# Wide products in the block passes of w1, a shared bank for two narrow ones, and weight sums made four steps at a time

## The chip, the cores and the metric

The kernel runs on one core of one Trainium2 chip. The time is device time in microseconds (us). Three runs of the kernel before took 515.21, 515.64 and 515.76 us; their median, 515.64 us, is the time before.

## The reference

The reference has two residual blocks over x (2048 tokens of 512 channels). The first is a linear attention with 32 heads; it is the same in both kernels. The second mixes tokens:

```
h  = x + attention(layernorm(x))
u  = gelu(w1^T · layernorm(h) + b1)       # w1: 2048 x 1792
h2 = h + (w2^T · u + b2)                  # w2: 1792 x 2048
```

All data are fp32. Every matmul operand is split into a high part (rounded to the type that TensorE takes, fp32r) and a low part (the rest), and a product is made of three: high with high, high with low, low with high.

## The kernel before

After the attention, the kernel walks through 96 numbered steps (`STEPS`). A step takes one tile of weights: 2 blocks of 128 rows by 256 columns. Steps 0 to 7 are pass 2 of w1, a plain one (kind "v"); steps 8 to 31 are passes 3, 4 and 5, the block passes (kind "u"), 8 steps each; steps 32 to 39 are pass 6, plain again; steps 40 to 95 are w2's (kind "y"). Passes 0 and 1 of w1 are filled in between the attention's work. This document is about steps 8 to 31.

In a block pass the 2x2 block product of a step is made of 7 products of 128x128 weights with 256 columns (a Winograd form of Strassen's scheme, P1 to P7) instead of 8. For that the weights need sums: of the 4 loaded blocks (slots 1 to 4 of `wraw`), VectorE makes slots 0, 5 and 6 and a new slot 1, four adds (`w_sums`, L801, L802, L803, L805), for two steps at a time. Then `w_parts` splits all 7 slots: ScalarE writes the high part (L66), VectorE subtracts it for the low part (L67), into one of three rotating tiles `wp` (`ws[n % 3]`). The activations have their sums too (`h_sums`, L738 and L739; `h_parts`, tiles `cb`), made for the last token tiles while the passes already run.

TensorE's work of a step is `products`: seven calls of `narrow`, each three matmuls of 256 columns (L989). They accumulate over the 8 steps of a pass into four PSUM banks a, b, c and d of 512 columns: P1 and P6 share a, P5 and P4 share b, P3 and P2 share c, P7 has the first half of d. Even and odd passes use different banks: an even pass takes the four of pool `ps_b`, an odd one two of `ps_f` and two of `ps_q`. At a pass's end `u_out` combines the banks: one copy on ScalarE (L1018) and five operations on VectorE (L1019 to L1028). Two steps later comes the gelu (L1033).

`wide`, which w2's steps use for four of their seven products, does the same product in two matmuls: the high weights with 512 columns (high and low activations side by side, L996), and the low weights with 256 (L998). It needs a whole bank for one product.

The order of everything is written by hand: all engines take their instructions in the order in which the program lists them. Step n runs `step(n)` (TensorE), then what is listed for n - 0.5, then `prepare(n + 2)`, which is `w_parts(n + 2)` and perhaps `w_sums`, then what is listed for n:

```python
for j, n in enumerate((0, 1, 2, 3, 5, 9, 12), 1):
    at(n - 1.5 if j > 3 else n - 0.5, h_sums, j)
    at(n, h_parts, j)
```

`U_ADDS` lists the steps at which the sums of a finished pass's u are made: two or three copies on ScalarE (L950), then a transfer that adds, issued by GpSimd (L951).

Of the kernel before, what the change touches and what calls it, by code (L numbers as in the profile page):

```python
# [9 lines left out]
F32 = mybir.dt.float32  # L10
F32R = mybir.dt.float32r
AF = mybir.ActivationFunctionType
ALU = mybir.AluOpType
# [4 lines left out]
P = 128  # L18
S, D, H, DH, F = 2048, 512, 32, 16, 1792
# [14 lines left out]
PLAIN = 2  # L34
KINDS = "vuuuv"
HD = D // 2
# [6 lines left out]
def block_kernel(ctx: ExitStack, tc: tile.TileContext, x, xT, wT, phic, wo, w1, b1, w2, b2,  # L43
                 kvmask, ident_in, out):
    nc = tc.nc
# [710 lines left out]
    Y0 = (NP - PLAIN) * (NT // 2)  # L756
# [36 lines left out]
    def w_sums(g):  # L793

        if 2 * g >= len(STEPS) or STEPS[2 * g][0] == "v":
            return
        plain = STEPS[2 * g][0] == "y"
        raw = BLOCK[g // 2 % 2] if plain else RAW[g]
        added = ADDED(2 * g)
        if not added:  # L800
            nc.vector.tensor_add(raw[:, :, 0], raw[:, :, 3], raw[:, :, 1])  # L801
        nc.vector.tensor_add(raw[:, :, 5], raw[:, :, 0], raw[:, :, 2])  # L802
        nc.vector.tensor_add(raw[:, :, 6], raw[:, :, 4], raw[:, :, 5])  # L803
        if not added:
            nc.vector.tensor_add(raw[:, :, 1], raw[:, :, 1], raw[:, :, 2])  # L805
# [10 lines left out]
        split(PARTS[n][0][:, k], PARTS[n][1][:, k], RAW[n // 2][:, n % 2, k], nc.vector)  # L816

    CB_FIRST = (0, 1, 2, 3)
    U_ADDS = {0: (5, 7, 9), 1: (6, 8, 10), 2: (11, 13, 15), 3: (19, 21, 23), 4: (28, 30, 32), 5: (34, 35.5, 37)}
    HELD = (44,)  # L820
    T_WORK = {5: 39.5}
    U_WORK = {0: 26, 1: 28, 2: 30, 3: 32, 4: 34, 5: 38, 6: 41}
# [162 lines left out]
    def narrow(o, n, m, x, opens, closes):  # L985

        wh_, wl_ = PARTS[n]
        for i, (w, y) in enumerate(((wh_, 0), (wh_, 1), (wl_, 0))):
            nc.tensor.matmul(o, w[:, m[0]], x[:, y], start=opens and i == 0, stop=closes and i == 2, skip_group_check=True)  # L989

    def wide(n, x, first, last, *products):


        wh_, wl_ = PARTS[n]
        for o, m in products:
            nc.tensor.matmul(o, wh_[:, m[0]], x(m[1]), start=first, stop=False, skip_group_check=True)  # L996
        for o, m in products:
            nc.tensor.matmul(o[:, 0], wl_[:, m[0]], x(m[1])[:, 0], start=False, stop=last, skip_group_check=True)  # L998
# [4 lines left out]
    def new_bank(pool):  # L1003
        return pool.tile([P, 2, HD], F32, name="py", tag="pu")

    def four_banks(i):
        return [new_bank(q) for q in ((ps_b,) * 4, (ps_f, ps_f, ps_q, ps_q))[i]]

    def products(n, banks, x, first, last):
        a, b, c, d = banks  # L1010
        for o, m, opens in ((a[:, 0], P1, True), (a[:, 1], P6, False), (d[:, 0], P7, True), (b[:, 0], P5, True),
                            (b[:, 1], P4, False), (c[:, 0], P3, True), (c[:, 1], P2, False)):
            narrow(o, n, m, x(m[1]), first and opens, last)

    def firsts(banks):
        a, b, c, d = banks
        tmp = wqp.tile([P, 4, HD], F32, name="tmp", tag="small")
        nc.scalar.activation(tmp[:, 1], a[:, 0], AF.Copy)  # L1018
        nc.vector.tensor_sub(tmp[:, 2], a[:, 1], tmp[:, 1])  # L1019
        nc.vector.tensor_sub(tmp[:, 3], tmp[:, 2], d[:, 0])  # L1020
        nc.vector.scalar_tensor_tensor(tmp[:, 0], b[:, 0], -1.0, tmp[:, 2], op0=ALU.mult, op1=ALU.subtract)
        return tmp[:, 0:2], tmp[:, 3].unsqueeze(1).to_broadcast([P, 2, HD])

    def u_out(p, banks):
        e, u3 = firsts(banks)
        U[p] = o = ur.tile([P, 4, HD], F32, name="u")
        nc.vector.tensor_add(o[:, 0:2], banks[1], u3)
        nc.vector.tensor_add(o[:, 2:4], banks[2], e)  # L1028

    def u_gelu(p):  # L1030
        for i in range(2):
# [9 lines left out]
    def wide_step(n, sp, p):  # L1041
        t = 2 * sp
        if p == 0:
            b3, b2 = [new_bank((ps_f, ps_q)[sp % 2]) for _ in range(2)]
            BK[:] = [new_bank(ps_b) for _ in range(4)] + [b3, b2]
        b16, b7, b5, b4, b3, b2 = BK
        first, end = p == 0, p == NP - 1

        def x(m):
            return UB[p, m]  # L1050

        def ws_(*products):
            wide(n, x, first, end, *products)

        w3, w2, w5, w4 = (b3, P3), (b2, P2), (b5, P5), (b4, P4)
        if first:
            ws_(w3, w2)
        elif not end:
            ws_(w3, w2, w5, w4)
        narrow(b16[:, 0], n, P1, x(1), first, end)  # L1060
        narrow(b16[:, 1], n, P6, x(5), False, end)
        narrow(b7[:, 0], n, P7, x(0), first, end)
        if first:
            ws_(w5, w4)
        if not end:
            return []
        ws_(w4, w5)
        ws_(w3, w2)
# [12 lines left out]
        nc.scalar.activation(lows[:, 3], b4[:, 1], AF.Copy)  # L1081
        tile_sum(0, 1, b4[:, 0], u3)
        add(l5, b5[:, 0], l5)
        add(e0, l5, u2)
        nc.scalar.activation(lows[:, 0], b3[:, 1], AF.Copy)  # L1085
        nc.scalar.activation(lows[:, 1], b2[:, 1], AF.Copy)
        tile_sum(0, 0, l5, u3)
        tile_sum(1, 0, b3[:, 0], e0, ALU.subtract)
        tile_sum(1, 1, b2[:, 0], e1)
        return [(t, 1, lows[:, 3:4]), (t, 0, ot[:, 0:2]), (t + 1, 0, ot[:, 2:4]), (t + 1, 0, lows[:, 0:2])]  # L1090

    def last_step(n, sp, p):
        t = 2 * sp
        if p == 0:
            b3, b2 = [new_bank((ps_f, ps_q)[sp % 2]) for _ in range(2)]
            BK[:] = [new_bank(ps_b) for _ in range(4)] + [b3, b2]
        b16, b7, b5, b4, b3, b2 = BK
        end = p == NP - 1
        if NP - 3 <= p < NP - 1:
            return []  # L1100
        places = [(b16[:, 0], P1, True), (b16[:, 1], P6, False), (b7[:, 0], P7, True), (b5[:, 0], P5, True),
                  (b4[:, 0], P4, True), (b3[:, 0], P3, True), (b2[:, 0], P2, True)]
        for o, m, opens in places if end else places[5:] + places[:5]:
            for k in range(2 if end else 0, -1, -1):
                narrow(o, n - k, m, UB[p - k, m[1]], opens and p == 0, end and k == 0)
        if end:
            last_sums(t, HB)
        return []
# [34 lines left out]
    def step(n):  # L1143

        kind, i, j = STEPS[n]
        if kind == "u":
            if j == 0:
                BANKS[0] = four_banks(i % 2)
            products(n, BANKS[0], lambda m: NB[j][m], j == 0, j == NT // 2 - 1)
            if j == NT // 2 - 1:  # L1150
                b = list(BANKS[0])
                later(0, lambda: u_out(i, b))
                later(2, lambda: u_gelu(i))
        elif kind == "v":
            if j == 0:
                PU[i] = [ps_b.tile([P, D], F32, name="pu", tag="pu") for _ in range(2)]
            wh_, wl_ = PARTS[n]
            for k in range(2):
                for c in range(2):
                    m, t = 1 + 2 * k + c, 2 * j + k  # L1160
                    mm3(PU[i][c], wh_[:, m], wl_[:, m], HN[t][:, 0], HN[t][:, 1], t == 0, t == NT - 1)
            if j == NT // 2 - 1:
                for c in range(2):
                    (later(0, lambda c=c: gelu(2 * i + c, PU[i][c])) if i < NP - 1 else gelu(2 * i + c, PU[i][c]))
        else:
            o = (last_step if i == NT // 2 - 1 else wide_step)(n, i, j)
            STORES.extend(o)
# [8 lines left out]
    def at(n, f, *args):  # L1176
        PENDING.setdefault(n, []).append(lambda: f(*args))

    for j, n in enumerate((0, 1, 2, 3, 5, 9, 12), 1):
        at(n - 1.5 if j > 3 else n - 0.5, h_sums, j)  # L1180
        at(n, h_parts, j)
    for p in range(PLAIN):
# [33 lines left out]
    def prepare(m):  # L1216

        if m >= len(STEPS):
            return
        w_parts(m)  # L1220
        made.add(m)
        if m >= Y0:
            if m % 4 == 2 and m > Y0 + 3:
                w_sums(m // 4 * 2 + 2)
        elif m % 2 == 0 and m + 2 < Y0:
            w_sums(m // 2 + 1)
        if m ^ 1 in made:
            load_raw(m // 2 + 4)
            add_raw(m // 2 + 3)
# [69 lines left out]
```

## Time and profile before

| | |
|---|---|
| time, median of three runs | 515.64 us |
| span of the profiled execution | 513.1 us |
| TensorE (PE) busy | 507.8 us, 99% |
| weight loads (PEld) busy | 441.7 us, 86% |
| VectorE (DVE) busy | 438.4 us, 85% |
| ScalarE (ACT) busy | 310.6 us, 61% |
| GpSimd (POOL) busy | 261.1 us, 51% |
| granted TensorE clock | 1.000 |

The span runs from the first to the last instruction of one profiled execution; the time of a run also holds what lies around the span. The profile has no time of its own for that execution beside its span; the median of the runs is 2.5 us above it. Busy time of PE counts matmuls that overlap, each for its whole length (0.28 us for one of 256 columns), so the distance between two starts, not the length, is what a matmul costs in a row of them.

### The profile page before, as it was taken

The page shows a single profiled execution, that of the slowest core. Times are in us where ns is not written, and L with a number is a line of the kernel's source. Part 1 is how long each engine was busy: PE and PEld are TensorE (multiplying, and loading weights), DVE is VectorE, ACT ScalarE, POOL GpSimd, SP SyncE. Part 2 cuts the span into 40 slices and gives each one's busy share as a digit, 9 for nine tenths or more (in the row PEclk, how much of TensorE's full clock was granted, in tenths as well). Part 3 has the DMA queues.
Part 4 walks back from the last instruction along what each step waited for, and adds up shares of the span by engine and source line. Part 5 has one row for each costly group of instructions (what it writes and reads, how often), then busy time and mean ns, then how long its engine had stood idle before and what let it go on. Part 6 is the DMA issues. An engine that isn't in the chain of part 4 may idle for free.

```text
span 513.1 us, 10496 instructions
## 1 busy us (share of the span) xinstructions
PE 507.8 (99%) x4024; PEld 441.7 (86%) x4024; DVE 438.4 (85%) x746; ACT 310.6 (61%) x557; POOL 261.1 (51%) x212
## 2 busy tenths in 40 slices
PE   8999999999999999999999999999999999999997
PEld 8888888888877777777788999998899999999997
DVE  6799889989887899699877898898799889868983
ACT  6999863525267878867676754577655444434530
POOL 3579997876999999985200421202323212211220
PEclk9999999999999999999999999999999999999999
DMA  8642301010123234354325775545677797668734
GB/s 308 217 144 84 103 22 42 1 65 21 42 64 103 67 100 145 127 169 132 95 69 185 150 159 125 133 115 151 173 164 147 181 199 167 122 153 190 169 51 85
DMA packets 53266, 63.35 MB, mean 123 GB/s; under 512 B 4832, under 2 KB 39904, under 8 KB 53216
## 3 DMA queue, kind: packets, MB, share of 16 engines
q1 hardware_dynamic: 44288, 51.90, 32.5%
q0 software_dynamic: 8640, 10.62, 14.9%
q8 instruction: 31, 0.51, 0.4%
q10 hardware_dynamic: 288, 0.17, 0.1%
q14 instruction: 19, 0.16, 0.1%
HBM read 48.39 MB, written 11.14 MB: 116 GB/s over the span
## 4 chain that ended last, share of the span: by engine, by line
PE 95%; DVE 2%; ACT 1%; DMA 1%; issue 0%; POOL 0%; DVEq 0%
PE py L989 25%; PE py L996 9%; PE pu L71 9%; PE pu L72 8%; PE pu L73 8%; PE py L998 4%; PE pk_ps L71 3%; PE pk_ps L72 3%; PE pk_ps L73 3%; PE pv L73 3%; PE pv L71 3%; PE pv L72 3%; PE po L71 3%; PE po L73 2%; PE po L72 2%; PE pn L616 2%
## 5 line engine op out<-in xcount | busy, mean ns | idle before, releaser
L66 ACT ACTIVATE wp<-wraw 128x896 fp32r<-128x896 f32 (+1 forms) x96 | 82.4, 895 | 68.3 <-DVE wraw L805 23.9
L67 DVE TENSOR_TENSOR wp<-wraw,wp 128x896 fp32r<-128x896 f32 (+1 forms) x96 | 95.5, 1019 | 14.9 <-ACT wp L66 14.6
L989 PE MATMUL py<-cb,wp 128*128 128x256 f32 x678 | 92.6, 283 | 0.0
L989 PEld LDWEIGHTS py<-cb,wp 128*128 128x128 f32 x678 | 86.1, 191 | 0.0
L1039 POOL DMA_DIRECT2D out<-u x28 | 24.8, 963 | 89.8 <-ACT u L1085 28.9
L951 POOL DMA_DIRECT2D tt<-u x14 | 13.4, 960 | 60.6 <-ACT tt L950 34.5
L490 POOL TENSOR_TENSOR ez<-eq,zB 128x1024 f32<-128x1024 f32 x16 | 38.4, 2406 | 3.8 <-ACT zB L550 3.8
L219 POOL TENSOR_TENSOR pk<-pk,sk 128x1024 f32<-128x1024 f32 x16 | 31.1, 1947 | 11.3 <-DVE sk L218 10.1
L996 PE MATMUL py<-cb,wp 128*128 128x512 f32 x126 | 36.1, 394 | 0.0
L514 POOL TENSOR_TENSOR eq<-eq,w 128x1024 f32<-128x1024 f32 x16 | 32.4, 2025 | 3.5 <-DVE w L511 3.5
L223 POOL TENSOR_TENSOR zacc<-zacc,pk 128x1024 f32<-128x1024 f32 x13 | 31.4, 2412 | 0.5
L989 PE MATMUL py<-hs,wp 128*128 128x256 f32 x216 | 30.0, 283 | 0.0
L989 PEld LDWEIGHTS py<-hs,wp 128*128 128x128 f32 x216 | 27.8, 192 | 0.1
L195 ACT ACTIVATE pk<-pk,r 128x1024 f32<-128x1024 f32 x16 | 18.4, 1149 | 15.0 <-DVE pk L173 14.4
L989 PE MATMUL py<-uf,wp 128*128 128x256 f32 x198 | 26.6, 283 | 0.0
L71 PE MATMUL pu<-wq,xs 128*128 128x512 f32 x64 | 26.1, 409 | 0.0
L71 PE MATMUL pu<-hs,whl 128*128 128x512 f32 x64 | 26.0, 406 | 0.0
L71 PE MATMUL po<-woh,oh 128*128 128x512 f32 x64 | 25.3, 396 | 0.1
L72 PE MATMUL pu<-wq,xs 128*128 128x512 f32 x64 | 25.0, 391 | 0.0
L73 PE MATMUL pu<-wq,xs 128*128 128x512 f32 x64 | 25.0, 390 | 0.0
L72 PE MATMUL pu<-hs,whl 128*128 128x512 f32 x64 | 25.0, 390 | 0.0
L73 PE MATMUL po<-woh,ol 128*128 128x512 f32 x64 | 25.0, 390 | 0.0
(226 smaller groups left out, 1422.1 us busy)
## 6 DMA issues: line engine op xcount, KB each, us to landing
wraw<-in_w SPq DMA_DIRECT2D x112, 256.0 KB, 3.4
out<-u POOLq DMA_DIRECT2D x21, 256.0 KB, 5.4
xraw<-in_xT SPq DMA_DIRECT2D x16, 256.0 KB, 2.9
xh<-in_x SPq DMA_DIRECT2D x16, 256.0 KB, 2.7
h<-in_x SPq DMA_DIRECT2D x16, 256.0 KB, 2.9
out<-h SPq DMA_DIRECT2D x16, 256.0 KB, 2.0
wraw<-in_wT SPq DMA_DIRECT2D x12, 256.0 KB, 4.9
tt<-u POOLq DMA_DIRECT2D x14, 128.0 KB, 3.8
```

The source lines that it names most:

```text
L66: nc.scalar.activation(hi, src, AF.Copy)
L67: lo_engine.tensor_sub(lo, src, hi)
L71: nc.tensor.matmul(o, ah, bh, start=first, stop=False)
L72: nc.tensor.matmul(o, ah, bl, start=False, stop=False)
L73: return nc.tensor.matmul(o, al, bh, start=False, stop=last).ins
L219: nc.gpsimd.tensor_mul(heads(PK[t]), heads(PK[t]), sk.unsqueeze(2).to_broadcast([P, 2 * H, DH]))
L223: nc.gpsimd.tensor_add(zacc, zacc, PK[t])
L490: nc.gpsimd.tensor_mul(EZ[t], EQ[t], zB)
L514: nc.gpsimd.tensor_mul(heads(EQ[t]), heads(EQ[t]), W[t].rearrange("p g c h -> p (g c h)").unsqueeze(2).to_broadcast([P, 2 * H, DH]))
L989: nc.tensor.matmul(o, w[:, m[0]], x[:, y], start=opens and i == 0, stop=closes and i == 2, skip_group_check=True)
L996: nc.tensor.matmul(o, wh_[:, m[0]], x(m[1]), start=first, stop=False, skip_group_check=True)
L1039: nc.gpsimd.dma_start(out[t * P:(t + 1) * P, k * HD:], flat(a), accum_op=ALU.add)
```

## The change

- `products` makes three of the seven products, P3, P2 and P4, with `wide`; the other four stay narrow. Each wide one has a bank of its own (b3, b2, b4); P1 and P6 share b16 as before, and P7 and P5 share b75. A pass's first step makes P3 and P2, then the narrow ones, then P4; the middle steps make the three wide ones first; the last step makes the narrow ones first.
- The five banks come as three of the four in `ps_b` for every block pass, and two of `ps_f` or `ps_q` in turn. Thus a block pass takes over two of its predecessor's three `ps_b` banks. Pass 6 (plain) takes its two banks from `ps_f` instead of `ps_b`, and w2's steps swap `ps_f` and `ps_q`.
- `u_out` has four copies on ScalarE instead of one (three of them read the second half of a wide bank) and eight operations on VectorE instead of five.
- `w_sums` always works on four steps at once, also in the block passes: it is called after `w_parts(m)` for m = 7, 11, 15, 19, 23 and 27, and sums the weights of steps m + 1 to m + 4.
- `h_parts(6)` is listed at step 10 instead of 9, which moves `h_sums(6)` from 7.5 to 8.5. Six entries of `U_ADDS` move by one step.

```diff
@@ w_sums
-        plain = STEPS[2 * g][0] == "y"
-        raw = BLOCK[g // 2 % 2] if plain else RAW[g]
+        raw = BLOCK[g // 2 % 2]
...
-    U_ADDS = {0: (5, 7, 9), 1: (6, 8, 10), 2: (11, 13, 15), 3: (19, 21, 23), 4: (28, 30, 32), 5: (34, 35.5, 37)}
+    U_ADDS = {0: (5, 8, 10), 1: (6, 9, 11), 2: (12, 14, 16), 3: (19, 21, 24), 4: (28, 30, 32), 5: (34, 35.5, 37)}
...
-    def four_banks(i):
-        return [new_bank(q) for q in ((ps_b,) * 4, (ps_f, ps_f, ps_q, ps_q))[i]]
+    def five_banks(pool):
+        b3, b2 = [new_bank(pool) for _ in range(2)]
+        return [new_bank(ps_b) for _ in range(3)] + [b3, b2]
...
+        def singles():
+            for o, m, opens in ((b16[:, 0], P1, True), (b16[:, 1], P6, False), (b75[:, 0], P7, True), (b75[:, 1], P5, False)):
+                narrow(o, n, m, x(m[1]), first and opens, last)
+
+        w3, w2, w4 = (b3, P3), (b2, P2), (b4, P4)
+        if last:
+            singles()
+            wide(n, x, first, last, w4, w3, w2)
+        elif first:
+            wide(n, x, first, last, w3, w2)
+            singles()
+            wide(n, x, first, last, w4)
+        else:
+            wide(n, x, first, last, w3, w2, w4)
+            singles()
+
+    def u_out(p, banks):
+        b16, b75, b4, b3, b2 = banks
...
+        nc.scalar.activation(e1, b16[:, 0], AF.Copy)
+        for k, b in ((1, b4), (2, b3), (3, b2)):
+            nc.scalar.activation(o[:, k], b[:, 1], AF.Copy)
+        sub(u2, b16[:, 1], e1)
+        sub(u3, u2, b75[:, 0])
+        nc.vector.scalar_tensor_tensor(e0, b75[:, 1], -1.0, u2, op0=ALU.mult, op1=ALU.subtract)
+        add(o[:, 0], b75[:, 1], u3)
+        add(o[:, 1], b4[:, 0], o[:, 1])
+        add(o[:, 2], b3[:, 0], o[:, 2])
+        add(o[:, 3], b2[:, 0], o[:, 3])
+        add(o[:, 1:4], o[:, 1:4], tmp[:, 0:3])
...
-    for j, n in enumerate((0, 1, 2, 3, 5, 9, 12), 1):
+    for j, n in enumerate((0, 1, 2, 3, 5, 10, 12), 1):
...
@@ prepare
-        elif m % 2 == 0 and m + 2 < Y0:
+        elif m % 4 == 3 and m + 1 < Y0:
             w_sums(m // 2 + 1)
```

Below, `hf` are the normalized activations, `wp` the weights' parts, `wraw` the loaded weights, `cb` the parts of the activations' sums, `py` the PSUM banks; a row with 128x896 handles the 7 slots of one step.

VectorE in pass 3, before, from the low part of step 11 to those of steps 13 and 14:

```order
L67 TENSOR_TENSOR wp<-wraw,wp 128x896
L67 TENSOR_TENSOR cb_3571<-hf,cb_3571 128x4x256
L67 TENSOR_TENSOR wp<-wraw,wp 128x896
L801 TENSOR_TENSOR wraw<-wraw 128x2x128
L802 TENSOR_TENSOR wraw<-wraw 128x2x128
L803 TENSOR_TENSOR wraw<-wraw 128x2x128
L805 TENSOR_TENSOR wraw<-wraw 128x2x128
L738 TENSOR_TENSOR hf<-hf 128x256 x2
L739 TENSOR_TENSOR hf<-hf 128x256 x2
L67 TENSOR_TENSOR wp<-wraw,wp 128x896 x2
```

The same place after; the row ahead of these holds the low parts of steps 8, 9 and 10:

```order
L738 TENSOR_TENSOR hf<-hf 128x256 x2
L739 TENSOR_TENSOR hf<-hf 128x256 x2
L67 TENSOR_TENSOR wp<-wraw,wp 128x896
L800 TENSOR_TENSOR wraw<-wraw 128x4x128
L801 TENSOR_TENSOR wraw<-wraw 128x4x128
L802 TENSOR_TENSOR wraw<-wraw 128x4x128
L804 TENSOR_TENSOR wraw<-wraw 128x4x128
L67 TENSOR_TENSOR wp<-wraw,wp 128x896
L67 TENSOR_TENSOR cb_3571<-hf,cb_3571 128x4x256
L738 TENSOR_TENSOR hf<-hf 128x256 x2
L739 TENSOR_TENSOR hf<-hf 128x256 x2
L67 TENSOR_TENSOR wp<-wraw,wp 128x896 x2
```

The sums of steps 12 to 15 now stand together, between the low parts of steps 11 and 12; the `hf` sums of j = 6 (first two rows), which stood ahead of step 10's low part, follow it.

VectorE at the end of pass 3, before, from the low part of step 17 to that of step 18 and the sums behind it:

```order
L67 TENSOR_TENSOR wp<-wraw,wp 128x896
L1019 TENSOR_TENSOR tmp<-py,tmp 128x256
L1020 TENSOR_TENSOR tmp<-tmp,py 128x256
L1021 SCALAR_TENSOR_TENSOR tmp<-py,tmp 128x256
L1027 TENSOR_TENSOR u<-py,tmp 128x512
L1028 TENSOR_TENSOR u<-py,tmp 128x512
L67 TENSOR_TENSOR wp<-wraw,wp 128x896
L801 TENSOR_TENSOR wraw<-wraw 128x2x128
```

The same place after, from the low parts of steps 16 and 17 to those of steps 18 and 19:

```order
L67 TENSOR_TENSOR wp<-wraw,wp 128x896 x2
L1037 TENSOR_TENSOR tmp<-py,tmp 128x256
L1038 TENSOR_TENSOR tmp<-tmp,py 128x256
L1039 SCALAR_TENSOR_TENSOR tmp<-py,tmp 128x256
L1040 TENSOR_TENSOR u<-py,tmp 128x256
L1041 TENSOR_TENSOR u<-py,u 128x256
L1042 TENSOR_TENSOR u<-py,u 128x256
L1043 TENSOR_TENSOR u<-py,u 128x256
L1044 TENSOR_TENSOR u<-u,tmp 128x768
L67 TENSOR_TENSOR wp<-wraw,wp 128x896 x2
```

The pass's end has three more operations, and the sums that stood right behind step 18's low part now come behind step 19's.

TensorE at the first steps of pass 4 after (before, each step is 21 matmuls of L989):

```order
L995 MATMUL py<-hs,wp 128x512 x2
L997 MATMUL py<-hs,wp 128x256 x2
L988 MATMUL py<-hs,wp 128x256 x3
L988 MATMUL py<-cb_3447,wp 128x256 x9
L995 MATMUL py<-cb_3447,wp 128x512
L997 MATMUL py<-cb_3447,wp 128x256
L995 MATMUL py<-hs,wp 128x512 x2
L995 MATMUL py<-cb_3448,wp 128x512
L997 MATMUL py<-hs,wp 128x256 x2
L997 MATMUL py<-cb_3448,wp 128x256
L988 MATMUL py<-hs,wp 128x256 x3
L988 MATMUL py<-cb_3448,wp 128x256 x9
```

The first six rows are step 16: P3 and P2 wide, the four narrow products, P4 wide; the other six are step 17, where the three wide ones stand first.

More of the change, by code (lines that the diff above doesn't have):

```diff
@@ L1004, in new_bank @@
         return pool.tile([P, 2, HD], F32, name="py", tag="pu")
-    def four_banks(i):
-        return [new_bank(q) for q in ((ps_b,) * 4, (ps_f, ps_f, ps_q, ps_q))[i]]
+    def five_banks(pool):
+        b3, b2 = [new_bank(pool) for _ in range(2)]
+        return [new_bank(ps_b) for _ in range(3)] + [b3, b2]
     def products(n, banks, x, first, last):
[L1010 to L1013, printed above, removed]
@@ L1015, in firsts @@
-    def firsts(banks):
-        a, b, c, d = banks
-        tmp = wqp.tile([P, 4, HD], F32, name="tmp", tag="small")
[L1018 to L1025, printed above, removed]
-        U[p] = o = ur.tile([P, 4, HD], F32, name="u")
-        nc.vector.tensor_add(o[:, 0:2], banks[1], u3)
-        nc.vector.tensor_add(o[:, 2:4], banks[2], e)
+        b16, b75, b4, b3, b2 = banks
@@ new lines, in u_out @@
+    def u_out(p, banks):
+        b16, b75, b4, b3, b2 = banks
+        tmp = wqp.tile([P, 4, HD], F32, name="tmp", tag="small")
+        u3, e0, e1, u2 = [tmp[:, k] for k in range(4)]
+        U[p] = o = ur.tile([P, 4, HD], F32, name="u")
+        add, sub = nc.vector.tensor_add, nc.vector.tensor_sub
+        nc.scalar.activation(e1, b16[:, 0], AF.Copy)
[9 more added lines that the diff above has]
+        add(o[:, 1:4], o[:, 1:4], tmp[:, 0:3])
@@ L1043, in wide_step @@
         if p == 0:
-            b3, b2 = [new_bank((ps_f, ps_q)[sp % 2]) for _ in range(2)]
+            b3, b2 = [new_bank((ps_q, ps_f)[sp % 2]) for _ in range(2)]
             BK[:] = [new_bank(ps_b) for _ in range(4)] + [b3, b2]
@@ L1094, in last_step @@
         if p == 0:
-            b3, b2 = [new_bank((ps_f, ps_q)[sp % 2]) for _ in range(2)]
+            b3, b2 = [new_bank((ps_q, ps_f)[sp % 2]) for _ in range(2)]
             BK[:] = [new_bank(ps_b) for _ in range(4)] + [b3, b2]
@@ L1147, in step @@
             if j == 0:
-                BANKS[0] = four_banks(i % 2)
+                BANKS[0] = five_banks((ps_f, ps_q)[i % 2])
             products(n, BANKS[0], lambda m: NB[j][m], j == 0, j == NT // 2 - 1)
@@ L1155, in step @@
             if j == 0:
-                PU[i] = [ps_b.tile([P, D], F32, name="pu", tag="pu") for _ in range(2)]
+                PU[i] = [(ps_f if i > PLAIN else ps_b).tile([P, D], F32, name="pu", tag="pu") for _ in range(2)]
             wh_, wl_ = PARTS[n]
```

## The prediction

> **What bounds the kernel now.** I read the page first, then the busy time in three stretches that are the three block passes, then the chain of waits in order of time, and last the timelines of PE, ACT and DVE around them.
>
> ```profile
> span 513.1 us, 10496 instructions
> PE 507.8 (99%) x4024; PEld 441.7 (86%) x4024; DVE 438.4 (85%) x746; ACT 310.6 (61%) x557; POOL 261.1 (51%) x212
> 288.47:308.63 20.16, 20.16 (x170) 20.16 (x169) 19.27 (x34) 13.03 (x21) 7.56 (x9) 1.00 0.76 163
> 308.63:328.78 20.15, 20.15 (x170) 20.15 (x169) 16.81 (x31) 10.47 (x15) 2.91 (x5) 1.00 0.56 134
> 328.78:348.94 20.16, 20.16 (x170) 20.16 (x169) 19.19 (x30) 14.21 (x21) 3.37 (x4) 1.00 0.48 122
> 288.63 60.47 PE py L989 x504
> 288.47 0.52 PE L989 MATMUL py<-hs,wp 128*128 128x256 f32 x3
> ```
>
> The first two lines are the page's: TensorE is busy for 99% of the span. The next three are the passes (busy us of PE, weight loads, DVE, ACT and POOL, each with its count): PE and the weight loads fill each pass completely, so in steps 8 to 31 no engine keeps TensorE waiting. The chain says the same: 504 matmuls in a row, 60.47 us for 24 steps, or 2.52 us a step and 0.120 us a matmul of 256 columns. So a gain can come from TensorE's own rate alone, and a loss from any wait that appears. DVE is the engine to fear: it is busy 19.27 of 20.16 us in pass 3. Step n starts at 288.47 + 2.52 (n - 8).
>
> **What wide products give.** Four wide and three narrow products stand in a step of w2:
>
> ```profile
> 395.44 1.09 PE L996 MATMUL py<-cb,wp 128*128 128x512 f32 x4
> 396.37 0.63 PE L998 MATMUL py<-cb,wp 128*128 128x256 f32 x4
> 396.84 1.24 PE L989 MATMUL py<-cb,wp 128*128 128x256 f32 x9
> 397.91 0.40 PE L996 MATMUL py<-cb,wp 128*128 128x512 f32 x1
> ```
>
> Four matmuls of 512 columns take 0.93 us from start to start (0.2325 each), four of 256 with the low weights 0.47 (0.1175), the nine narrow ones 1.07. A wide product costs 0.350 us, a narrow one 0.360; and this step takes 2.47 us where a narrow one takes 2.52, which is 0.0125 for each wide product. The change has 3 x 24 = 72 of them: 0.7 to 0.9 us, and I take 0.8. A step then takes 2.485 us. This is all that the change can win, and it is less than 0.2% of the time (1.0 us, about what a measurement of this kernel can tell from no change).
>
> The Trainium skill, page "TensorE: Matmul & The Clock Gate", section "Back-to-back issue gap", gives N / 2.4 + 2.5 ns for one matmul's distance; that is an estimate of 327.6 ns for a narrow and 325.0 for a wide product, a gain of 0.2 us over 72 and a forecast 0.6 us later than mine. The rows above differ from it (120 ns where it has 109), and the rows decide.
>
> **What the moved sums cost.** The high part of a step (ACT) reads the slots that the sums write, the low part (DVE) needs the high part, and TensorE needs both. Before, sums of two steps stood a step and more ahead of their use. Now four steps' sums end just ahead of the high part of the first of the four, and DVE idles until that is done. The prices:
>
> ```profile
> 289.25 0.94 ACT L66 ACTIVATE wp<-wraw 128x896 fp32r<-128x896 f32 x1
> 290.23 1.09 DVE L67 TENSOR_TENSOR wp<-wraw,wp 128x896 fp32r<-128x896 f32 x1 [0.37 <-ACT wp L66]
> 291.24 0.42 DVE L801 TENSOR_TENSOR wraw<-wraw 128x256 f32<-128x256 f32 x1
> 292.83 1.08 DVE L67 TENSOR_TENSOR wp<-wraw,wp 128x896 fp32r<-128x896 f32 x1
> 297.56 0.88 DVE L738 TENSOR_TENSOR hf<-hf 128x256 f32<-128x256 f32 x2
> 299.27 2.08 DVE L67 TENSOR_TENSOR wp<-wraw,wp 128x896 fp32r<-128x896 f32 x2
> 302.86 1.22 DVE L67 TENSOR_TENSOR cb<-hf,cb 128x1024 fp32r<-128x1024 f32 x1
> 304.00 2.08 DVE L67 TENSOR_TENSOR wp<-wraw,wp 128x896 fp32r<-128x896 f32 x2
> 311.39 0.95 ACT L66 ACTIVATE wp<-wraw 128x896 fp32r<-128x896 f32 x1 [1.56 <-PE py L989]
> 430.26 0.68 DVE L805 TENSOR_TENSOR wraw<-wraw 128x512 f32<-128x512 f32 x1
> 431.11 2.64 ACT L66 ACTIVATE wp<-wraw 128x896 fp32r<-128x896 f32 x3 [4.38 <-DVE wraw L805]
> 435.18 0.69 DVE L801 TENSOR_TENSOR wraw<-wraw 128x512 f32<-128x512 f32 x1
> 437.24 0.68 DVE L805 TENSOR_TENSOR wraw<-wraw 128x512 f32<-128x512 f32 x1
> ```
>
> A low part of 7 slots: 1.09 us, the next operation 1.01 after its start (290.23 to 291.24). Four hf sums: 1.71 (297.56 to 299.27). A cb low part: 1.14 to the next. Sums of two steps: 1.59 to the next (291.24 to 292.83); of four: 2.06 from the first start to the last, and 0.68, is 2.74 to the result (the rows at 435.18 and 437.24). ACT starts a high part 0.17 after the sums end (430.94 to 431.11); it takes 0.95; DVE starts 0.03 after it.
>
> *Step 13.* The high part of step 10 ends at 290.20 in both, since on ACT the gelu of pass 2, which needs step 7's end, stays ahead of it. From there DVE's queue in its new order: low part of step 10 at 290.23, the hf sums of j = 6 (moved behind it, they leave DVE idle ahead of it) at 291.24, low part of 11 at 292.95, sums of 12 to 15 at 293.96, ended at 296.70. High part of 12: 296.87 to 297.82, DVE idle for over a microsecond. Low part of 12 at 297.85, cb at 298.86, hf sums of j = 7 at 300.00, low part of 13 from 301.71 to 302.80. TensorE starts step 13 at 288.47 + 5 x 2.485 = 300.90 and needs its low weights after three matmuls of 512 columns, at 301.60: a wait of 1.2 us. Before, the same low part ended at 300.36 (299.27 + 1.09) and step 13 began at 301.07, so the spare was 0.7.
>
> *Step 16, the pass's seam.* DVE has no gap up to there: low parts of 13 and 14, cb and low part of 15 bring it to 305.88, sums of 16 to 19 to 308.62, high part of 16 until 309.74, low part until 310.86. TensorE is at step 16 at 288.47 + 8 x 2.485 + 1.2 = 309.55 and needs the low weights two wide matmuls (0.465) later: 0.85 of waiting. Then banks:
>
> ```profile
> 302.45 0.40 ACT L950 ACTIVATE u<-u 128x256 f32<-128x256 f32 x1
> 302.75 0.40 ACT L950 ACTIVATE tt<-tt 128x256 f32<-128x256 f32 x1
> 308.60 0.42 DVE L1019 TENSOR_TENSOR tmp<-py,tmp 128x256 f32<-128x256 f32 x1
> 309.12 0.42 DVE L1020 TENSOR_TENSOR tmp<-tmp,py 128x256 f32<-128x256 f32 x1
> 309.45 0.42 DVE L1021 SCALAR_TENSOR_TENSOR tmp<-py,tmp 128x256 f32<-128x256 f32 x1
> 309.79 0.68 DVE L1027 TENSOR_TENSOR u<-py,tmp 128x512 f32<-128x512 f32 x1
> 338.80 0.95 DVE L67 TENSOR_TENSOR cb<-tt,cb 128x768 fp32r<-128x768 f32 x1
> ```
>
> P7 of the new pass writes the bank that was b16 in the old one; it is free when L1037, the first of `u_out` on DVE, has read it. Ahead of that stands the low part of 17, whose high part comes behind that of 16 and two `U_ADDS` copies (0.30 each by the first two rows): 309.65 + 0.60 + 0.95 + 0.03 = 311.23, and L1037 ends at 312.66. TensorE is there at 310.86 + 2 x 0.1175 + 6 x 0.12 = 311.81: 0.85 more. P4 then writes the old b75, free after L1040, which starts 1.19 after L1037 (308.60 to 309.79) and ends at 313.85; TensorE is there at 313.38: 0.47. Step 16 loses 2.2 us. Without the copies ahead it would lose 1.6.
>
> *Steps 20 to 29.* `u_out` goes on with three adds (0.34 each) and one of 768 columns (0.95, the row at 338.80) to 315.75; low parts of 18 and 19, then sums of 20 to 23 until 320.5, high part to 321.6, low part to 322.75. TensorE, at step 17 from 314.2, needs it at 314.2 + 3 x 2.485 + 0.70 = 322.35: 0.4. The same rows laid on give 0.2 at step 24 (the bank of P4), 0.4 at step 28 and 0.5 at 29 (the parts of pass 0's u stand on DVE there). These 1.5 us are the least certain: from 0, if TensorE's own lateness lets DVE recover, to 3. In a quiet round the new order holds: ACT starts 0.25 after step 4k+1 begins (the row at 311.39; step 17 began at 311.15), and 0.95 + 0.03 + 1.01 + 2.74 + 0.17 + 0.95 + 0.03 + 1.09 later, at 7.22, the low part of step 4k+4 is there, and is needed at 3 x 2.485 + 0.47 = 7.93.
>
> *What costs nothing.* The three further ACT copies (0.38 us each at most, by the copy rows) lie in ACT's idle time, 7 us a pass; they delay the high part of step 18 by a microsecond, which waits for DVE anyway. Pass 6 takes the banks that pass 4 left, eight steps free; w2's first steps take pass 5's, eight steps free too. The transfers of the raw weights are issued when the low part eight steps back is done, and land in 3.4 us (the second row of the fence below). After step 31 no weights are summed until w2, and TensorE runs on as before, later by the sum.
>
> **The sum.** Waits 1.2 + 2.2 + 0.4 + 1.1 = 4.9, gain 0.8: 4.1 us more. The span goes from 513.1 to 517.2; the median lies 2.5 above the span and I add the same: 515.64 + 4.1 = 519.7 us.
>
> **The rivals.**
>
> *No wait lands, and the kernel is faster (0.14).* DVE makes the sums of four steps in 2.66 us to the next operation instead of 2 x 1.59, half a microsecond less a round, and a low part is needed 0.46 us later in a step than before (after three wide matmuls, not two narrow ones). If that covers step 13, which decides at a low part ready by 301.60, the rest has a lighter load, and the time is 515.64 - 0.8 = 514.8. Against it: 1.2 us are missing there, and pass 3 left DVE only 0.9 us idle.
>
> *Only the first wait stays (0.12).* TensorE's lateness of 1.2 us gives DVE the time to be ready at step 16 and after: 515.64 - 0.8 + 1.2 = 516.0, within 0.2%. Against it: the queue laid out above runs without a gap from step 12's low part to the sums of 16, so it gains nothing from the wait.
>
> *ACT waits as well (0.06).* The `U_ADDS` copy of step 16 waits for a transfer issued only after ACT's copies at 310.2:
>
> ```profile
> tt<-u POOLq DMA_DIRECT2D x14, 128.0 KB, 3.8
> wraw<-in_w SPq DMA_DIRECT2D x112, 256.0 KB, 3.4
> ```
>
> At the median of 3.8 us to landing it is free about when DVE is; at 5 us the high part of step 19 and with it step 20 come a microsecond later, and step 24's copy likewise: 521 to 521.5.
>
> **How the numbers follow.** The forecast, waits at steps 13 and 16 and some behind, has 0.68: 517.6 to 521.2 us, by the bounds of its least certain term (0 to 3) and of step 16 (1.6 to 2.2), and 519.7 as laid out. The range of 515.5 to 522.0 takes in the one-wait rival and the one with ACT, and leaves out the faster one (514.8) and little else. Faster by over 0.2% (under 514.6) needs more than the 0.8 us that I find: 0.05, from the first rival. Within 0.2% (514.6 to 516.7): the rest of the first rival and nearly all of the second, 0.18. Slower: 0.77.
>
> **What would show it.** Right: PE idle ahead of step 13's first L997 and ended by DVE's L67; idle ahead of the fourth L988 of step 16's second group and of its L995, ended by L1037 and L1040; DVE idle over a microsecond ahead of the low parts of steps 12, 16, 20 and 28, ended by ACT's L66; the block passes 64 to 65 us long instead of 60.47, with matmuls that cost 0.2325 and 0.1175 us between waits. Wrong: block passes of 59.6 us with PE full, which is the first rival, or a low part of step 13 that ends by 301.6.

## The result: 5 us slower, and where they went

| | before | after |
|---|---|---|
| time, median of four runs each | 515.70 us (515.21 to 515.94) | 520.86 us (520.76 to 521.50) |
| ratio, with its 95% interval | | 1.0105 (1.009 to 1.0119) |
| span of the profiled execution | 513.1 us | 519.1 us |
| time of the profiled execution | not shown | 520.87 us |

The forecast was 519.7 us, in a range of 515.5 to 522.0; the change is slower by 1%. The page of after (its first line and that of busy time), then busy us of PE, weight loads, DVE, ACT and POOL in its three block passes, cut where TensorE starts steps 8, 16, 24 and 32:

```profile
span 519.1 us, 10342 instructions
PE 510.4 (98%) x3952; PEld 438.2 (84%) x3952; DVE 438.9 (85%) x731; ACT 312.3 (60%) x566; POOL 261.0 (50%) x212
288.45:309.82 21.37, 20.27 (x145) 18.65 (x143) 16.89 (x25) 11.31 (x19) 6.07 (x7) 1.00 0.66 143
309.82:333.33 23.51, 21.34 (x147) 18.98 (x145) 18.38 (x26) 12.55 (x23) 5.21 (x6) 1.00 0.55 124
333.33:354.39 21.06, 20.67 (x146) 18.73 (x145) 19.70 (x28) 15.42 (x26) 3.04 (x4) 1.00 0.47 123
```

PE filled every pass before; now it stands idle for 1.1, 2.2 and 0.4 us of them, and the passes take 65.94 us instead of 60.47. That is 5.5 of the span's 6.0 us. DVE is less busy than before in pass 3 (16.89 us against 19.27), so a lack of DVE time is not the reason there; the experiments show that the order of its work is. The waits of PE in the whole span (engine, line and what it waited for; us in total, times, longest), without two rows of 1.1 and 0.2 us that before has too:

```profile
PE py L997 <- DVE wp L67: 1.9, 4, 1.1
PE py L995 <- ACT wp L66: 0.8, 1, 0.8
PE py L988 <- DVE tmp L1037: 0.6, 1, 0.6
PE py L995 <- DVE u L1040: 0.2, 1, 0.2
```

None of them was there before. From the timelines of PE and DVE, the places: first the wait in step 13, then the three of step 16.

```profile
297.91 1.09 DVE L67 TENSOR_TENSOR wp<-wraw,wp 128x896 fp32r<-128x896 f32 x1 [1.15 <-ACT wp L66]
301.77 2.08 DVE L67 TENSOR_TENSOR wp<-wraw,wp 128x896 fp32r<-128x896 f32 x2
302.91 0.51 PE L997 MATMUL py<-hs,wp 128*128 128x256 f32 x2 [1.10 <-DVE wp L67]
309.81 1.09 DVE L67 TENSOR_TENSOR wp<-wraw,wp 128x896 fp32r<-128x896 f32 x1 [1.16 <-ACT wp L66]
310.95 0.50 PE L997 MATMUL py<-hs,wp 128*128 128x256 f32 x2 [0.39 <-DVE wp L67]
312.27 0.42 DVE L1037 TENSOR_TENSOR tmp<-py,tmp 128x256 f32<-128x256 f32 x1
312.74 0.98 PE L988 MATMUL py<-cb,wp 128*128 128x256 f32 x6 [0.58 <-DVE tmp L1037]
313.46 0.41 DVE L1040 TENSOR_TENSOR u<-py,tmp 128x256 f32<-128x256 f32 x1
313.93 0.50 PE L995 MATMUL py<-cb,wp 128*128 128x512 f32 x1 [0.21 <-DVE u L1040]
```

The first and the fourth row are the pattern: behind four steps' sums DVE stands idle for 1.15 us, until ACT has made the high part from them. The idle time in brackets counts from the modelled end of the former matmul, so it is less than the step loses. What a step loses is the distance between its first matmul and the next step's, less 2.487 us, the distance in undisturbed steps (2.52 in kernels with narrow products alone):

| | forecast, us | measured, us |
|---|---|---|
| step 13 | 1.2 | 1.37 |
| step 16 (low part, L1037, L1040) | 2.2 | 2.08 |
| steps 19 and 20 | 0.4 | 0.99 + 0.54 |
| step 24 | 0.2 | 0.27 |
| steps 28 and 29 | 0.4 + 0.5 | 0.39 + 0.51 |
| wide products, 24 steps | -0.8 | -0.8 (24 x (2.487 - 2.52)) |
| w2's steps 46 and 47 | 0 | 0.51 |

TensorE is level with before at step 8, 5.45 us late at step 32, and 6.0 us late from step 60 to the end.

The row that is far off is that of step 20. From the timelines of POOL, ACT, DVE and PE, in order of time:

```profile
310.99 1.19 POOL L950 DMA_DIRECT2D tt<-u  x1
316.62 0.42 ACT L949 ACTIVATE tt<-tt 128x256 f32<-128x256 f32 x1 [3.46 <-DMA tt<-u]
316.94 0.94 ACT L66 ACTIVATE wp<-wraw 128x896 fp32r<-128x896 f32 x1
317.91 1.09 DVE L67 TENSOR_TENSOR wp<-wraw,wp 128x896 fp32r<-128x896 f32 x1 [1.05 <-ACT wp L66]
318.92 0.69 DVE L800 TENSOR_TENSOR wraw<-wraw 128x512 f32<-128x512 f32 x1
322.81 2.09 DVE L67 TENSOR_TENSOR wp<-wraw,wp 128x896 fp32r<-128x896 f32 x2 [1.15 <-ACT wp L66]
322.83 0.73 PE L995 MATMUL py<-hs,wp 128*128 128x512 f32 x2 [0.83 <-ACT wp L66]
```

The transfer is issued at 310.99 and lands 5.6 us later; the copy listed at step 16 (L949) waits 3.46 us for it, and the high part of step 19 stands behind the copy. DVE idles 1.05 us for that high part with the sums of 20 to 23 behind it, idles 1.15 us more for the high part of 20, and TensorE arrives before even the high part is there: the 0.99 us booked to step 19 are the wait at the head of step 20.

### The profile page after: what moved, and what is told of

It reads as the page before. It is cut to its first block, busy times and chain, and to the rows that moved or that the text cites. A ratio compares the mean times of both kernels' runs of the same rounds, so it can differ in the third digit from the quotient of the medians.

```text
span 519.1 us, 10342 instructions
## 1 busy us (share of the span) xinstructions
PE 510.4 (98%) x3952; PEld 438.2 (84%) x3952; DVE 438.9 (85%) x731; ACT 312.3 (60%) x566; POOL 261.0 (50%) x212
## 4 chain that ended last, share of the span: by engine, by line
PE 80%; DVE 8%; issue 4%; ACT 4%; DMA 3%; POOL 0%; DVEq 0%; ACTq 0%; POOLq 0%
PE py L988 13%; PE py L995 8%; PE pu L71 8%; PE pu L72 7%; PE pu L73 7%; PE py L997 4%; PE pk_ps L71 3%; PE pk_ps L72 3%; PE pv L71 3%; PE pk_ps L73 3%; PE pv L72 3%; PE pv L73 3%; PE po L71 3%; PE po L73 2%; PE po L72 2%
## 5 line engine op out<-in xcount | busy, mean ns | idle before, releaser
L67 DVE TENSOR_TENSOR wp<-wraw,wp 128x896 fp32r<-128x896 f32 (+1 forms) x96 | 95.2, 1020 | 21.1 <-ACT wp L66 20.8
L988 PE MATMUL py<-cb,wp 128*128 128x256 f32 x606 | 84.2, 283 | 0.6 <-DVE tmp L1037 0.6
L988 PEld LDWEIGHTS py<-cb,wp 128*128 128x128 f32 x606 | 77.4, 191 | 0.8 <-DVE tmp L1037 0.8
L995 PE MATMUL py<-cb,wp 128*128 128x512 f32 x150 | 45.9, 397 | 0.2 <-DVE u L1040 0.2
L995 PEld LDWEIGHTS py<-cb,wp 128*128 128x128 f32 x150 | 25.7, 190 | 3.5 <-DVE u L1040 0.6
L997 PE MATMUL py<-cb,wp 128*128 128x256 f32 x150 | 28.3, 279 | 0.0
L997 PEld LDWEIGHTS py<-cb,wp 128*128 128x128 f32 x150 | 25.2, 188 | 3.6
L71 PE MATMUL pu<-wq,xs 128*128 128x512 f32 x64 | 26.1, 409 | 0.0
L71 PE MATMUL pu<-hs,whl 128*128 128x512 f32 x64 | 25.9, 405 | 0.0
L988 PEld LDWEIGHTS py<-uf,wp 128*128 128x128 f32 x198 | 25.0, 191 | 0.3 <-DVE uf L67 0.3
L72 PE MATMUL pu<-wq,xs 128*128 128x512 f32 x64 | 25.0, 390 | 0.0
L72 PE MATMUL po<-wol,oh 128*128 128x512 f32 x64 | 25.0, 390 | 0.0
```

What stands on the lines that cost most here:

```text
L67: lo_engine.tensor_sub(lo, src, hi)
L71: nc.tensor.matmul(o, ah, bh, start=first, stop=False)
L72: nc.tensor.matmul(o, ah, bl, start=False, stop=False)
```

## Experiments

Two theories are named in the expectations. **A, the order of the queues:** TensorE waits for low and high parts because of what stands ahead of them on DVE and ACT. **B, the banks:** the wide products, with five banks and a longer `u_out`, are what costs. Lag means TensorE's start of a step against the same step of before; step 8 itself starts up to 0.6 us apart in these executions. Runs told with a ratio were timed beside before on the same chip.

**1. The new order without wide products.** Before, with only the order of after:

```diff
-        plain = STEPS[2 * g][0] == "y"
-        raw = BLOCK[g // 2 % 2] if plain else RAW[g]
+        raw = BLOCK[g // 2 % 2]
...
-    U_ADDS = {0: (5, 7, 9), 1: (6, 8, 10), 2: (11, 13, 15), 3: (19, 21, 23), 4: (28, 30, 32), 5: (34, 35.5, 37)}
+    U_ADDS = {0: (5, 8, 10), 1: (6, 9, 11), 2: (12, 14, 16), 3: (19, 21, 24), 4: (28, 30, 32), 5: (34, 35.5, 37)}
...
-    for j, n in enumerate((0, 1, 2, 3, 5, 9, 12), 1):
+    for j, n in enumerate((0, 1, 2, 3, 5, 10, 12), 1):
...
-        elif m % 2 == 0 and m + 2 < Y0:
+        elif m % 4 == 3 and m + 1 < Y0:
```

The change moves eight entries of `U_ADDS` by a step, as the diff shows; the six given above are a miscount.

> The kernel before with the sums of four steps, the hf sums of j = 6 and the U_ADDS of the changed one; products, banks and the pass's end stay narrow. Theory A (the waits come from the order of VectorE's queue: sums of four right ahead of their use, hf sums of j = 6 behind step 10): TensorE waits about 1.3 us at step 13, 0.5 at step 16, 1 to 2.4 at step 20, 3.5 to 5 in all, and the time is 519.2 to 520.7 us. Theory B (the waits come from the banks that a pass takes over from its predecessor and from the longer pass's end): no wait, 515.7 us.

Measured: 521.77 us against 515.74, ratio 1.0113 (1.0097 to 1.013). In its timelines, the same place as above, and then TensorE in two stretches of 3.41 us around step 20 (length, busy time of PE, weight loads, DVE, ACT and POOL, granted clock):

```profile
298.52 1.09 DVE L67 TENSOR_TENSOR wp<-wraw,wp 128x896 fp32r<-128x896 f32 x1 [1.16 <-ACT wp L66]
303.52 0.39 PE L988 MATMUL py<-hs,wp 128*128 128x256 f32 x1 [1.08 <-DVE wp L67]
320.83:324.25 3.42, 1.71 (x13) 1.30 (x11) 2.27 (x3) 1.98 (x3) 0.00 (x0) 1.00 0.21 66
324.25:327.66 3.41, 3.26 (x15) 3.26 (x16) 2.10 (x3) 0.96 (x2) 0.86 (x1) 0.50 0.63 135
```

With the old products and the old banks the order alone costs as much as the whole change: steps 12 and 13 lose 1.7 us, step 16 0.5, steps 19 and 20 4.2, step 29 0.2. Some 1.6 us of those 4.2 (half of 3.26) are the half clock of the last row, which after does not have. This execution is the slowest of the four, 522.08 us at a mean clock of 0.995; the one at 1.000 took 520.70, the upper end of what A allowed. B is refuted as the main cause; at step 16, where this kernel loses 0.5 and after 2.08, the wide products' banks have a part (2 and 5 below).

**2. Wide products without the new order of sums.** After, with sums of two steps at the old places and `h_parts(6)` at 9:

```diff
-        raw = BLOCK[g // 2 % 2]
+        raw = BLOCK[g // 2 % 2] if STEPS[2 * g][0] == "y" else RAW[g]
...
-    for j, n in enumerate((0, 1, 2, 3, 5, 10, 12), 1):
+    for j, n in enumerate((0, 1, 2, 3, 5, 9, 12), 1):
...
-        elif m % 4 == 3 and m + 1 < Y0:
+        elif m % 2 == 0 and m + 2 < Y0:
```

> The changed kernel with its wide products, banks, pass's end and U_ADDS, but with sums of two steps and the hf sums of j = 6 as before. Theory A: the wait at step 13 and those at 20, 28 and 29 are gone, at most 0.4 us is left at step 16; steps of 2.487 us are kept; 514.9 to 515.4 us (515.7 - 0.8 + 0 to 0.4). Theory B: the 2.1 us at step 16 and the 0.3 at step 24 stay: about 517.3 us.

Measured: 516.27 us (514.61 to 519.34, 10 runs), ratio 1.0012 (0.9995 to 1.0029). The profiled execution is the slowest of the ten. Its block passes lose 0.59 us at step 16 (P4's bank, which L1040 frees; before, with the same sums and narrow products, does not wait there) and nothing anywhere else; TensorE's lag is 0.17 at step 8 and 0.01 at step 32. But w2's opening waits, in step 54:

```profile
PE py L988 <- DVE u L1094: 2.8, 1, 2.8
405.28:408.69 3.41, 0.90 (x6) 0.61 (x5) 3.26 (x5) 2.14 (x6) 0.01 (x1) 1.00 0.63 89
408.69:412.10 3.41, 3.09 (x12) 2.90 (x13) 3.14 (x9) 2.69 (x4) 0.85 (x1) 0.50 0.78 180
```

The waits of 13, 20, 28 and 29 are gone with the old places, as A has it; at step 16 a little more than A's 0.4 is left. The median lies in neither theory's place, since step 54 was in neither: it loses 4.5 us in this execution, 1.5 of them (half of 3.09) to a stretch at half clock. That is a second matter, taken up in 6.

**3. One term alone: step 13.** After, with `h_parts(6)` at step 9, so that the `hf` sums of j = 6 stand ahead of step 10's low part again:

```diff
-    for j, n in enumerate((0, 1, 2, 3, 5, 10, 12), 1):
+    for j, n in enumerate((0, 1, 2, 3, 5, 9, 12), 1):
```

> The changed kernel with the hf sums of j = 6 listed as before (h_parts(6) at step 9). Theory A: the wait of 1.37 us at step 13 is gone, step 16 keeps 1.5 to 1.7 of its 2.1; the span is shorter by 1.7 to 2.0 us: about 517.3 where the changed kernel has 519.1. Theory B: only the wait at step 13 goes, by what it was, and step 16 keeps 2.1: 517.7.

One run: 519.76 us, span 518.0. Step 13 loses nothing, step 16 1.52 instead of 2.08, steps 19 and 20 the same 0.99 + 0.54, 24 to 29 the same (and step 54 of w2's opening 0.9, see 6). From step 8 to step 32 TensorE takes 63.92 us instead of 65.94, the 2.0 that A gave; the span is only 1.1 shorter, since step 8 starts 0.5 later in this execution and step 54 waits.

The edit moves two things, the `hf` sums of j = 6 (1.7 us) and the `cb` low part made from them (1.14 us to the next operation). The second row here stands behind the low part of step 12 in after, and now fills the gap that the four sums leave:

```profile
295.74 0.68 DVE L804 TENSOR_TENSOR wraw<-wraw 128x512 f32<-128x512 f32 x1
296.34 1.22 DVE L67 TENSOR_TENSOR cb<-hf,cb 128x1024 fp32r<-128x1024 f32 x1
297.58 1.09 DVE L67 TENSOR_TENSOR wp<-wraw,wp 128x896 fp32r<-128x896 f32 x1
```

So the later place of `h_parts(6)` makes the whole of step 13's wait, and a quarter of step 16's. Which of its two parts does it was not tried. An estimate from after's rows: with the `hf` sums alone moved back, the low part of 11 could start when its high part ends, 0.9 us earlier (292.1 instead of 293.01), which does not cover 1.37.

**4. One term alone: step 20.** The three entries of `U_ADDS` for a pass run one, two and one copies, each followed by its transfer. After, with the last copy of pass 2 listed two steps later:

```diff
-    U_ADDS = {0: (5, 8, 10), 1: (6, 9, 11), 2: (12, 14, 16), 3: (19, 21, 24), 4: (28, 30, 32), 5: (34, 35.5, 37)}
+    U_ADDS = {0: (5, 8, 10), 1: (6, 9, 11), 2: (12, 14, 18), 3: (19, 21, 24), 4: (28, 30, 32), 5: (34, 35.5, 37)}
```

> The kernel after, with one copy of U_ADDS listed at step 18 instead of 16 (the one on ScalarE that waits for pass 2's adding transfer). Theory (the 1.5 us at steps 19 and 20 come from ScalarE, whose queue stands behind that copy until the transfer has landed at 316.6): the waits at steps 19 and 20 fall from 1.5 to about 0.4 to 0.5 us, which are VectorE's own; a little less at step 16, because one copy less stands ahead of step 17's high part (L1037 wait 0.6 to 0.3 us); the other waits stay; the span is 1.0 to 1.4 us shorter than the 519.1 of after: 517.7 to 518.2. Rival (VectorE's queue alone makes the wait at step 20): steps 19 and 20 still lose 1.5 us and the span stays within 0.3 us of 519.1.

One run: 524.07 us, span 522.3. From the timelines of ACT and DVE, and then PE and the granted clock in w2's opening:

```profile
314.59 0.95 ACT L66 ACTIVATE wp<-wraw 128x896 fp32r<-128x896 f32 x1 [1.43 <-PE py L997]
399.52 0.69 DVE L801 TENSOR_TENSOR wraw<-wraw 128x512 f32<-128x512 f32 x1 [1.84 <-DMA wraw<-in_w]
408.16 0.69 DVE L800 TENSOR_TENSOR wraw<-wraw 128x512 f32<-128x512 f32 x1 [3.10 <-issue]
413.54 2.11 PE L988 MATMUL py<-cb,wp 128*128 128x256 f32 x9 [3.05 <-DVE u L1094]
410.36:413.77 3.41, 0.36 (x4) 0.23 (x3) 3.15 (x5) 2.69 (x7) 0.56 (x1) 1.00 0.58 130
413.77:417.19 3.42, 3.42 (x15) 3.13 (x15) 3.25 (x8) 2.14 (x3) 0.31 (x1) 0.50 0.63 129
```

The high part of step 19 starts at 314.59 instead of 316.94, steps 19 and 20 lose 0.37 instead of 1.53, and every other wait of the block passes is as in after: the lag at step 32 is 4.32 instead of 5.45. That is the theory's figure for step 20, and the rival is out. The "little less at step 16" did not come (2.07): the copies ahead of step 17's high part are the two of the entry before, which did not move. The expected span was missed, since w2's opening lost 4.9 us in this execution. The kernel as a whole settles nothing; the stretch does.

**5. The sums one step earlier, alone and with the other two repairs.** After, with

```diff
-        elif m % 4 == 3 and m + 1 < Y0:
+        elif m % 4 == 2 and m + 2 < Y0:
```

> The changed kernel with its sums of four steps called one step earlier (behind the low part of step 4k+2 instead of 4k+3), nothing else. Theory A: the high part of step 4k+4 no longer waits for them; 0.2 us of waiting stay at step 11, 1.2 at step 15 (the hf sums stand in the way) and up to 0.5 at 19, none at 13, 16, 20, 24, 28 and 29: 516.3 to 517 us. Theory B: the waits at steps 16 and 24 stay, 517.5 us or more.

Measured: 517.59 us (517.30 to 517.62), ratio 1.0038 (1.0023 to 1.0053). Two rows of its waits:

```profile
PE py L988 <- DVE wp L67: 0.9, 1, 0.9
PE py L988 <- DVE u L1094: 1.3, 1, 1.3
```

The block passes lose 0.22 in step 11 and 1.16 in step 15 and nothing else: the seams, step 16's banks too, are clear, and the lag at step 32 is 0.69. The second row is w2's opening again, where step 54 loses 1.75 us. The time alone, 517.59, is what B gave; the places show that A holds in the block passes and that the rest was lost behind them. With `h_parts(6)` at 9 and the old places in `U_ADDS` as well, but for pass 2's last copy (16 instead of 15) and pass 3's (24 instead of 23) (`0: (5, 7, 9)`, `1: (6, 8, 10)`, `2: (11, 13, 16)`):

> The kernel after with the weights' sums of four steps listed one step earlier (after w_parts of m = 6, 10, 14, 18, 22 and 26), h_parts(6) back at step 9, and U_ADDS of before but for the one at 23 or 24. Theory (every wait in steps 8 to 31 is a matter of what stands ahead of a low part in VectorE's and ScalarE's queues; wide products and shared banks cost nothing of their own): no wait of over 0.3 us in steps 8 to 31, 2.485 us a step, TensorE 0.8 us earlier than before at step 32; a median of 514.9 us if w2's opening (steps 46 to 54) does not wait, and up to 519 if it waits for its transfers as in the runs with less delay ahead of it. Rival 1 (sums of four steps are too much for VectorE at any place): 1 us or more of waits at step 13 or 16, 516.5 or later with w2's opening without a wait. Rival 2 (the shared banks cost a wait of their own at each seam): 0.5 us or more at steps 16 and 24, ended by L1037 or L1040.

Measured: 515.53 us (514.23 to 517.78, 12 runs), ratio 0.9987 (0.9966 to 1.0007). Its block passes, cut at even stretches of 19.88 us, and DVE and PE in w2's opening:

```profile
288.40:308.28 19.88, 19.88 (x145) 18.83 (x144) 18.64 (x26) 12.73 (x21) 6.88 (x8) 1.00 0.76 154
308.28:328.16 19.88, 19.88 (x146) 18.75 (x145) 16.88 (x25) 11.03 (x18) 3.47 (x4) 1.00 0.60 145
328.16:348.04 19.88, 19.88 (x146) 18.75 (x146) 19.52 (x28) 15.22 (x25) 3.42 (x4) 1.00 0.48 122
401.28 0.69 DVE L800 TENSOR_TENSOR wraw<-wraw 128x512 f32<-128x512 f32 x1 [1.68 <-issue]
406.66 1.10 PE L988 MATMUL py<-cb,wp 128*128 128x256 f32 x7 [1.29 <-DVE u L1094]
403.50:406.90 3.40, 2.11 (x14) 1.69 (x13) 3.14 (x5) 2.70 (x7) 1.23 (x2) 1.00 0.79 132
```

PE is busy throughout, as before. From the first matmul of step 8 to that of step 32 it takes 59.75 us instead of 60.47, so a pass is 19.92 us, a little longer than these stretches: the wide products win 0.72 us (the lag goes from -0.08 to -0.80), sums of four fit, and five banks cost nothing once the queues are clear. Rivals 1 and 2 are out. The gain is lost again in step 54, 1.7 us in this execution.

**6. W2's opening.** There DVE sums the weights of four steps at a time. For steps 48 to 55 (`ADDED`) two slots of the sums come from accumulating loads that GpSimd issues; the next raw loads, while stores of `out` are under way as well, land 3 to 6 us after their issue. DVE takes its work in order, so it waits for them, and L1094, which frees a bank for step 54, stands two low parts and four sums behind. The same kernel with fewer of these loads:

```diff
-        return n in () or n - Y0 in range(8, 16)
+        return n in () or n - Y0 in range(8, 12)
```

> The kernel before this one in the list, with VectorE making the weights' sums of steps 52 to 55 itself, instead of by accumulating loads that GpSimd issues (four accumulating loads and four plain ones fewer in w2's opening). Theory (w2's opening waits because accumulating loads and plain loads land late while TensorE comes early): the wait at step 54 is gone, the block passes are as in the kernel without this edit, and the median is 514.9 us, with less spread between runs than the 4.7 us of the wide kernel with sums of two. Rival (the wait at step 54 is VectorE's load, not the transfers): four more sums on VectorE, 2.7 us, make it longer, and the median is 517 or more.

Measured: 514.53 us (514.15 to 515.62, 12 runs) against 515.62 for 29 runs of before on that chip; ratio 0.9968 (0.9951 to 0.9985). DVE at the loads, and PE in step 54:

```profile
400.75 0.69 DVE L800 TENSOR_TENSOR wraw<-wraw 128x512 f32<-128x512 f32 x1 [0.86 <-DMA wraw<-in_w]
406.14 1.34 PE L988 MATMUL py<-cb,wp 128*128 128x256 f32 x9
```

DVE has one short wait left, step 54 loses 0.5 us instead of 1.7, and the twelve runs lie within 1.5 us where those of the kernel without this edit spread over 3.6. Of the 1.2 us between the two executions, 0.7 are that TensorE comes later here, as it did at step 8 already; the other 0.5 are that L1094 starts earlier (405.67 instead of 406.19), behind raw loads that took 3.0 to 4.1 us instead of 4.7 to 5.6. So the rival is out (the median is not 517, and DVE's four more sums did not make the wait longer), and the theory fits, though the wait did not go to zero and one execution of each is all that shows it. As a control, before with that last edit alone:

> The kernel before with that last edit alone (sums of steps 52 to 55 made by VectorE). A control: TensorE does not wait in w2's opening in the kernel before, so taking loads from there should give nothing: 515.7 us, within 0.2%. If it is slower by over 1 us, VectorE has no room for these sums in w2's opening, and the rival of the kernel before it in the list holds.

Measured: 515.08 us (514.93 to 516.78, 10 runs), ratio 0.9977 (0.9954 to 0.9999). That is within the 0.2% expected, at the fast end, and its interval only just leaves out no change. Step 54 loses 0.5 us in its profiled execution, where the profiled one of before loses nothing; the 29 runs of before lie between 514.85 and 520.01 us, so it probably waits somewhere there in some executions too, but no trace shows that. The difference between the last two kernels, 514.53 and 515.08, is 0.55 us, near the 0.72 that the wide products win, but their runs overlap. The kernel with all the edits beats before by 0.15 to 0.5%, and after by some 1.4% (1.0105 over 0.9968).

## Why the prediction was right, and where it was off

*Wide products.* Right: 0.8 us forecast; 24 x 0.033 in after, 0.72 in the kernel without waits. By the Trainium skill, page "TensorE: Matmul & The Clock Gate", section "Back-to-back issue gap", whose formula is for an isolated matmul, the estimate was 0.2; the trace bears out its own rows (0.2325 and 0.1175 to 0.12 us between starts), not the page's figures.

*Step 13.* Right in place, cause and size. The low part was forecast to end at 302.80 and ended at 302.85; the remaining 0.1 is a restart that was not counted: the first two matmuls of 256 columns after the wait lie 0.17 us apart instead of 0.12 (302.91 to 303.25 for the two). Experiment 3 shows that the later place of `h_parts(6)`, with its `hf` sums and its `cb` part, is what makes it.

*Step 16.* Right: 2.08 for 2.2, in the three parts that were named, by L67, L1037 and L1040. L1037 started at 312.27 (312.24 by the working).

*Step 20.* The step of the prediction that failed in size: 0.4 forecast, 1.53 measured. The forecast took 3.8 us to landing, the median over the whole kernel, for the transfer ahead of the `U_ADDS` copy; it took 5.6, and it was issued at 310.99, behind another one at 310.44, where the forecast counted from ACT's copies at 310.2. The third rival had named this very mechanism, "at 5 us the high part of step 19 and with it step 20 come a microsecond later", and had 0.06 for it; its 521 to 521.5 is nearer to the result than the forecast itself. Experiment 4 shows that the copy is the cause. A chance of 0.06 was too low. In the block passes of before the adding transfers land in 2.6 to 5.4 us. This one is issued half a microsecond behind another of them (310.44, landed in 4.5) and at the same time as a raw load (310.92), and it took 5.6 here, 5.6 in experiment 3 and 5.4 in experiment 4. Two of before had the same neighbours, those at 288.09 and 291.33, and took 4.4 and 5.4. So it is no chance outlier, and the trace of before held a better price: a single transfer that an engine waits for should be priced by what is issued beside it, at the slow end of its kind, not by the kernel's median.

*Steps 24 to 29.* Right within 0.1 us each, though called the least certain. That TensorE's "own lateness lets DVE recover" did not come about, since DVE idles its 1.15 us for the high part in a round however late TensorE comes.

*After step 31.* "TensorE runs on as before, later by the sum" was wrong by 0.5 us: w2's opening has a chain of loads, DVE sums and L1094 with little spare. It cost 0.5 us in after, and between nothing and 4.9 in the experiments, with no relation to the lag: 4.5 at a lag of 0, 4.9 at 4.3, 0.5 at 5.4 (after), nothing at 7.2 (experiment 1). What decides in which execution the loads come late is not settled.

*From span to time.* The span grew by 6.0 us, the median by 5.2. The 2.5 us that the prediction put between them was the distance of before's median from a profiled execution whose own time is not shown. The experiments' profiled executions lie 1.8 to 2.1 above their spans, and after's 1.8; so before's profiled execution was probably one of some 515 us, under its median. By luck this took 0.7 off the two misses above; without it the forecast would have been 1.9 us short instead of 1.2.

*The rivals.* "No wait lands" and "only the first wait stays" are out by the first table. Experiment 5 shows how near the first of them was: with the sums one step earlier and seven other steps in the lists moved, no wait lands.

## What to carry to other kernels

Where several engines share one handwritten order, a batch of work that makes another engine's input should not be the last thing ahead of its use: here the same four adds cost nothing one step earlier, once the lists around them were back at their old places too, and 1.15 us of DVE's time each round where they stood. Lay the new order out row by row with durations from the trace, for every engine that is waited for; that gave five of the six places named within 0.2 us, and what it missed were transfers, which should be priced by the slow cases among those that run beside others. Judge an edit by the stretch that it touches, since a later stretch with little spare (here w2's opening, up to 4.9 us) can hide or invert what the edit did.

## What the runs showed of the hardware

TensorE's clock falls to one half inside a full kernel after a wait that is not long at all. In three runs it stood at 0.50 for a stretch of 3.41 us, each time right behind a stretch of 3.41 us in which PE was busy for 1.71, 0.90 and 0.36 us (experiments 1, 2 and 4); where PE was busy for 2.11 of 3.40 us (experiment 5, cut at the same beat of 3.41 us counted from the grant of the full clock) it stayed at 1.00. At the end of experiment 5's first kernel a stretch with 1.83 us busy (510.25 to 513.66) left it at 1.00 too, so here the limit lies between 1.71 and 1.83 us busy. Half of the busy time in the slow stretch is lost, 1.5 to 1.7 us in these three runs, on top of the wait itself; the wait of 1.29 us in experiment 5 cost nothing beyond itself. The Trainium skill, page "TensorE: Matmul & The Clock Gate", section "Part 1: The HAM clock gate (the "warmup" mystery)", gives a window of 3413 ns and has the clock fall after at least one idle window; the length agrees with these rows, but the window need not be idle: 1.71 of 3.42 us busy was not enough to keep the clock.

An adding transfer of 128 KB takes longer in some company, in a way that repeats: the one issued at the seam of passes 3 and 4, half a microsecond behind another and within half a microsecond of a raw load of 256 KB, took 5.4 to 5.6 us in after and in experiments 1 to 4, and 4.5 in the first kernel of experiment 5, where the fastest of the block passes of before took 2.6. A neighbour of its own kind alone does not do it: the second ones of the pairs at 303.76 in before and 330.13 in after, with no raw load issued within a microsecond, took 3.0 and 2.8. Whether the raw load alone does was not tried.
